# An attention and feed-forward kernel whose order is a table of times: two entries moved by a fifth of a pair

## The chip, the cores and the metric

The kernel runs on one core of one Trainium2 chip. The metric is the device time of one execution in microseconds (us); the runs of the kernel before took 1797.93, 1798.88 and 1799.62, median 1798.88. A further execution of it was profiled; the trace is of that one.

The engines of the core are called PE (TensorE, the matrix unit; PEld is its loading of weights), VectorE or DVE, ScalarE or ACT, GpSimd or POOL, and SyncE or SP, which issues the transfers. Each works through its own instructions in the order in which the program issued them, and waits where an operand or a buffer is not ready.

## What is computed

`x` holds 4 batches of 12480 tokens of 128 features. The first step is attention of 32 learned points over all tokens of a batch, the second is attention of the tokens over the 32 results, and the third is a feed-forward with a squared ReLU of width 2048.

```python
def mab(q, kv):
    s = scale * (q @ kv.transpose(0, 2, 1))
    s = s - s.max(-1, keepdims=True)
    a = np.exp(s)
    a /= a.sum(-1, keepdims=True) + 1e-09
    return a @ kv
h = mab(I, x)
attn = mab(x, h)
...
h = np.maximum(attn @ w_in, 0.0)
return (h * h @ w_out)
```

## The kernel before

The tokens of a batch come in 13 *units* of 960, each in two *blocks* of 480. A block goes through the feed-forward in eight *pairs* of 128-wide slices of the 2048. For each pair of a block (function `ffn_block`, line numbers of the profile):

- `wide` (L508): two matmuls into `h` in PSUM, from `hw`, the product of the attention's result and `w_in`, and `st`, the attention weights.
- `relu` (L515) and `square` (L522) on ScalarE make `r` and then `g`, 128 x 960.
- `high` (L593 on VectorE, L595 on GpSimd) rounds `g` to `hi`, in the PE's reduced float32; the table `HI` says which engine does it for which pair. For one pair in sixteen it says "f": that pair is not split.
- `low` (L530) on VectorE subtracts: `lo` = `g` - `hi`.
- `narrow` (L543): six matmuls add into `op` in PSUM: `hi` by `wo_hi` twice, `hi` by `wo_lo` twice, `lo` by `wo_hi` twice. The pair that is not split has two full float32 products of `g` by `wo_f` in their place.

After a block's last pair, `done` copies `op` to `ot` (VectorE, L593), `turn` transposes it on PE into `otp` (L569), `turned` scales it into `osb` (VectorE, L577), and after the second block `osb` is sent out.

Between these the attention runs ahead. Of the next unit, the second attention: `s` (PE, L420), `ss`, `s2t` (PE, L432), `mx`, `d` (VectorE, L443), the exponential on ScalarE, `sk` (GpSimd and VectorE), and `ap` (PE, L477), which becomes `st`. Of the next batch, the first attention: `xtp` (PE, L263), `sp` (L278), `ep` (L312), `hp` (L324). In a batch's last unit `first_end` joins the first attention's results and makes `hw` of the next batch out of four products `wp` (PE, L393). The last batch has no first attention beside it. All the small PE results share two PSUM banks (`bank`), which go round: the second `wp` takes the bank that `s2t` had, once `d` has read it.

Nothing is scheduled by a tool. Each step is entered in a list with a time on a clock that counts pairs, the list is sorted, and the steps are issued in that order:

```python
t = t0 + p
for i in range(2):
    at(t + AT_G1 + 0.01 * i, lambda i=i: wide(i))
at(t, relu)
...
    at(t + AT_HI[HI[k][p]], high)
    at(t + AT_LO, low)
for j in range(len(steps)):
    at(t + AT_G2 + AT_G2D * j * (6 // len(steps)), lambda j=j: narrow(j))
...
end = t0 + NP - 1 + AT_G2 + 6 * AT_G2D
```

So the table's numbers set no times on the chip; they only set which instruction stands ahead of which on its engine. The buffers go round as well: three of `r` and `lo`, four of `g` and `hi`, two of `h`.

Of the kernel before, what the change touches and what calls it, by code (L numbers as in the profile page):

```python
# [18 lines left out]
PSUM = bass.MemoryType.PSUM  # L19

P = 128
TS = 120          # tokens of a sub-tile
NT = 8            # sub-tiles of a unit
UNIT = TS * NT    # tokens of a unit
BLK = UNIT // 2   # tokens of a block, the width of the feed-forward products


@with_exitstack
def induced_attention_then_squared_relu_ffn(
# [9 lines left out]
    B, N, C = x.shape  # L39
# [3 lines left out]
    NP = NF // 2  # L43
    NU = N // UNIT
    Q = P // M
    scale = 1.0 / math.sqrt(C)
    # engines, by pair of f-tiles in the first and the second block of a unit; "f": not split
    SQ = ('aaaaaaaa', 'aaaaaaaa')   # of the square
    HI = ('vpvpvvpf', 'vvpvvpvv')   # of the rounding
    # engines that empty PSUM  # L50
    XT, XT_EARLY, ET, SS, ST, OT = 'av', 'aa', 'a', 'v', 'av', 'vv'
    RB, GB, HB, LB = 3, 4, 4, 3
    AT_G1, AT_SQA, AT_SQV, AT_HIP, AT_HIA, AT_HIV, AT_LO, AT_G2, AT_G2D = -1.4, 1.05, 0.8, 1.1, 0.7, 1.2, 2.05, 3.3, 0.16
    AT_HI = {"p": AT_HIP, "a": AT_HIA, "v": AT_HIV}
    T_START = (-0.2, 0.3, 0.6, 0.7, 1.5, 1.7, 2.0, 2.4, 3.2, 3.3, 4.1, 4.5)
    T_MAIN = (1.1, 2.2, 2.9, 4.2, 7.2, 7.7, 8.02, 10.3, 10.5, 11.1, 13.4, 13.5)
# [20 lines left out]
    def bank(name):  # L77
        return ps_m.tile([P, 512], F32, tag="m", name=name)

    # token p * (N / TS) + j of a batch lies on partition p of sub-tile j  # L80
    x_v = x.rearrange("b (p j) c -> b p j c", p=TS)
    out_v = out.rearrange("(b p j) c -> b p j c", b=B, p=TS)

    def load_x(b, u, pool):
        xn = pool.tile([TS, NT, C], F32, tag="xn", name=f"xn_{b}_{u}")
        nc.sync.dma_start(xn, x_v[b, :, u * NT:(u + 1) * NT, :])
        return xn
# [4 lines left out]
    make_identity(nc, ident)  # L92
    identr = const.tile([P, P], F32R, name="identr")
    nc.vector.tensor_copy(identr, ident)
    # same_m[(q m), (k m')] = (m == m')
    same_m = const.tile([P, Q, M], F32, name="same_m")
    nc.vector.tensor_reduce(
        same_m[:, 0, :], ident.rearrange("p (q m) -> p m q", q=Q), axis=AX.X, op=ALU.add
# [2 lines left out]
        nc.vector.tensor_copy(same_m[:, k, :], same_m[:, 0, :])  # L101

    same = same_m.rearrange("p k m -> p (k m)")
    # lane_q[(q m), q'] = (q == q')
    lane_q = const.tile([P, Q], F32, name="lane_q")
    nc.vector.tensor_reduce(
        lane_q, ident.rearrange("p (q m) -> p q m", q=Q), axis=AX.X, op=ALU.add
# [6 lines left out]
    indT = const.tile([C, M], F32, name="indT")  # L114
    nc.vector.tensor_copy(indT, it_ps[:C, :M])

# [1 line left out]
    plan = []  # L118

    def at(t, fn):  # L120
# [2 lines left out]
    w_in_sb = const.tile([C, F], F32, name="w_in_sb")  # L123
    wo_hi = const.tile([P, NF, C], F32R, name="wo_hi")
    wo_lo = const.tile([P, NF, C], F32R, name="wo_lo")
    # w_out's tiles for the products that are not split
    FULL = [p for p in range(NP) if "f" in (HI[0][p], HI[1][p])]
    wo_f = const.tile([P, 2 * max(len(FULL), 1), C], F32, name="wo_f")

# [3 lines left out]
    ABOVE = float(np.array(1151 << 20, np.int32).view(np.float32))  # L133

    def weights(name, load, use, t0, step):
        """Steps that turn float64 weights, as words (low, high), into float32 parts (a, b).

        a has the leading 21 bits and b the rest; what float32 has no exponent for becomes 0 or
        infinite, as a cast would have it: a high word's order as a float32 is that of its exponent.
        """  # L140
        v = {}
        shape = [P, WCH]

        def tile_of(tag, dtype):
            return pools["stage"].tile(shape, dtype, tag=tag, name=f"{tag}_{name}")

        def words():
            v["w"] = pools["stage"].tile([P, WCH, 2], I32, tag="words", name=f"words_{name}")
            load(v["w"])

        def clamp():
            v["hc"] = tile_of("hc", F32)
            nc.vector.tensor_scalar(
                v["hc"], v["w"][:, :, 1].bitcast(F32), ABOVE, -ABOVE, ALU.min, ALU.max
            )

        def size():
            v["m"] = tile_of("m", F32)
            nc.scalar.activation(v["m"], v["hc"], AF.Abs)

        def flush():
            nc.vector.scalar_tensor_tensor(v["hc"], v["m"], LEAST, v["hc"], ALU.is_ge, ALU.mult)

        def field():
            v["a"] = tile_of("a", I32)
            nc.vector.tensor_scalar(
                v["a"], v["hc"].bitcast(I32), 3, 0x3FFFFFF8,
                ALU.logical_shift_left, ALU.bitwise_and,
            )

        def sign():
            nc.vector.scalar_tensor_tensor(
                v["a"], v["hc"].bitcast(I32), -0x40000000, v["a"], ALU.bitwise_and, ALU.bitwise_or
            )

        def power():
            v["power"] = tile_of("m", I32)
            nc.vector.tensor_single_scalar(v["power"], v["a"], -0x800000, ALU.bitwise_and)

        def low():  # L180
            v["b"] = tile_of("b", F32)
            nc.vector.scalar_tensor_tensor(
                v["b"], v["w"][:, :, 0].bitcast(U32), 2.0 ** -52, v["power"].bitcast(F32),
                ALU.mult, ALU.mult,
            )
            use(v["a"].bitcast(F32), v["b"])

        at(t0 - 1.5, words)
        for i, fn in enumerate((clamp, size, flush, field, sign, power, low)):
            at(t0 + step * i, fn)  # L190
# [4 lines left out]
        pools["stage"] = pools["scope"].enter_context(tc.tile_pool(name="stage", bufs=2))  # L195

    def open_ffn():
        """The feed-forward takes the place of the weights' staging."""
        pools["scope"].close()
        pools["ffn"] = ctx.enter_context(tc.tile_pool(name="ffn", bufs=3))  # L200

# [38 lines left out]

    state = {}

# [1 line left out]
    # lane (q m): inducing point m over the sub-tiles 2q and 2q + 1 of each unit  # L244
    def first_unit(b, u, t0, ahead, times, early=False):
        v = {}
        n = f"{b}_{u}"
        s = state.setdefault(b, {"xt": []})
# [4 lines left out]
        def turn(k):  # L253
            if k == 0:
                v["xt"] = xt_pool.tile([C, UNIT], F32, tag="xt", name=f"xt_{n}")
                s["xt"].append(v["xt"])
# [5 lines left out]
            for t in range(4):  # L262
                nc.tensor.transpose(  # L263
                    tp[:, t * TS:(t + 1) * TS], v["xn"][:, 4 * k + t, :], ident[:TS, :TS]
                )

        def turned(k):
            part = v["xt"][:, k * BLK:(k + 1) * BLK]
            copy((XT_EARLY if early else XT)[k], part, v["tp"][:, :BLK])

# [14 lines left out]
            nc.vector.tensor_reduce(v["mx"], v["sp"][:, :2 * TS], axis=AX.X, op=ALU.max)  # L285

        def shift():
            # the maximum so far, times -scale
            v["neg"] = tiny.tile([P, 1], F32, tag="neg", name=f"neg_{n}", bufs=4)
            if u:  # L290
                v["before"] = s["neg"]
                nc.vector.scalar_tensor_tensor(
                    v["neg"], v["mx"], -scale, s["neg"], ALU.mult, ALU.min
                )
            else:
                nc.vector.tensor_scalar_mul(v["neg"], v["mx"], -scale)
            s["neg"] = v["neg"]
# [50 lines left out]
            at(t0 + t, fn)  # L348

    def first_end(b, t0, times):  # L350
        """Joins the lanes of each inducing point; h transposed, four times, and h @ w_in split."""
        v = {}
        s = state[b]

# [50 lines left out]
        for t, fn in zip(times, fns):  # L405
            at(t0 + t, fn)

# [1 line left out]
    def second_unit(b, u, t0, times):  # L409
        """The unnormalised weights of a unit's tokens, split in two, as (hi, lo, hi, lo) on partitions."""  # L410
        v = {}
        n = f"{b}_{u}"
        s = state[b]
# [69 lines left out]
        def stacked(k):  # L483
            st = att.tile([P, BLK], F32R, tag="st", name=f"st_{n}_{k}", bufs=4)
            copy(ST[k], st, v["ap"][:, :BLK])
            s["st", u, k] = st
# [5 lines left out]
        for t, fn in zip(times, fns):  # L492
            at(t0 + t, fn)

# [1 line left out]
    def ffn_block(b, u, k, t0):  # L496
        n = f"{b}_{u}_{k}"
        s = state[b]
        w = {}

        def pair(p):
            v = {}

            def wide(i):
                if i == 0:
                    v["hp"] = ps_h.tile([P, 2, 512], F32, tag="h", name=f"h_{n}_{p}")
                f = 2 * p + i
                nc.tensor.matmul(  # L508
                    v["hp"][:, i, :BLK], s["hw"][:, f * P:(f + 1) * P], s["st", u, k],
                    start=True, stop=True,  # L510
                )

            def relu():
                v["r"] = pools["ffn"].tile([P, 2, BLK], F32, tag="r", name=f"r_{n}_{p}", bufs=RB)
                nc.scalar.activation(v["r"], v["hp"][:, :, :BLK], AF.Relu)  # L515
# [57 lines left out]
        def turned():  # L573
            if k == 0:
                s["osb", u] = att.tile([TS, NT, C], F32, tag="osb", name=f"osb_{b}_{u}")
            # block k holds the sub-tiles 2q + k
            nc.vector.tensor_mul(  # L577
                s["osb", u].rearrange("t (q k) c -> t k q c", k=2)[:, k],
                w["tp"][:TS, :].rearrange("t (q c) -> t q c", q=Q),
                s["zz", u][:, k * Q:(k + 1) * Q].broadcast_to([TS, Q, C]),  # L580
            )
            if k == 1:
                nc.sync.dma_start(out_v[b, :, u * NT:(u + 1) * NT, :], s["osb", u])

# [9 lines left out]
        else:  # L594
            nc.gpsimd.tensor_scalar(dst, src, 1.0, 0.0, ALU.mult, ALU.add)  # L595

    # batch 0's first attention, then per batch its blocks and the first attention of the next
    U = 2 * NP
    t_end = START * NU + T_END
    t_main = t_end + T_FFN  # L600
# [52 lines left out]
```

## Time and profile before

| | |
|---|---|
| median of three runs | 1798.88 us |
| span of the profiled execution | 1796.8 us |
| PE busy | 1766.7 us, 98% |
| ScalarE busy | 1628.0 us, 91% |
| VectorE busy | 1620.0 us, 90% |
| GpSimd busy | 442.8 us, 25% |
| mean granted clock of PE | 0.994 |

The span runs from the first to the last instruction; what a run takes beyond it is the start and the end around the program. In a row of the timeline stand the start and the time in us, the engine, the line, the operation, what is written and read (`out<-in`), partitions by elements, and a count; a bracket gives the idle time ahead of it and what ended it. PE's starts are the thing to read: its matmuls overlap, so a matmul's own time is longer than the distance to the next. A row of waits gives the total in us, how often, and the longest.

### The profile page before, as it was taken

The page shows a single profiled execution, that of the slowest core. Times are in us where ns is not written, and L with a number is a line of the kernel's source. Part 1 is how long each engine was busy: PE and PEld are TensorE (multiplying, and loading weights), DVE is VectorE, ACT ScalarE, POOL GpSimd, SP SyncE. Part 2 cuts the span into 40 slices and gives each one's busy share as a digit, 9 for nine tenths or more (in the row PEclk, how much of TensorE's full clock was granted, in tenths as well). Part 3 has the DMA queues.
Part 4 walks back from the last instruction along what each step waited for, and adds up shares of the span by engine and source line. Part 5 has one row for each costly group of instructions (what it writes and reads, how often), then busy time and mean ns, then how long its engine had stood idle before and what let it go on. Part 6 is the DMA issues. An engine that isn't in the chain of part 4 may idle for free.

```text
span 1796.8 us, 27067 instructions
## 1 busy us (share of the span) xinstructions
PE 1766.7 (98%) x9729; PEld 1422.9 (79%) x9729; DVE 1620.0 (90%) x2315; ACT 1628.0 (91%) x2070; POOL 442.8 (25%) x439
## 2 busy tenths in 40 slices
PE   7799999999999999999999999999999999999998
PEld 4478888888778888888878888888887888888887
DVE  6899989999989989989989989989989999999998
ACT  5699999999899999999988999999999999999997
POOL 1312222222222222222221222222222323233231
PEclk9899999999999999999999999999999999999999
DMA  8200100100100110100100110110100000000000
GB/s 214 57 23 23 44 23 23 45 23 23 45 23 23 37 31 23 45 23 23 45 23 23 28 39 23 35 33 23 38 19 12 23 12 23 12 16 19 12 23 23
DMA packets 16912, 57.07 MB, mean 32 GB/s; under 512 B 1704, under 2 KB 3784, under 8 KB 16776
## 3 DMA queue, kind: packets, MB, share of 16 engines
q1 hardware_dynamic: 16776, 55.34, 11.5%
q8 instruction: 76, 1.25, 0.3%
q14 instruction: 60, 0.49, 0.1%
HBM read 29.77 MB, written 25.56 MB: 31 GB/s over the span
## 4 chain that ended last, share of the span: by engine, by line
PE 95%; DVE 2%; DMA 1%; issue 0%; ACT 0%; SPq 0%; POOL 0%; ACTq 0%; DVEq 0%
PE op L543 62%; PE h L508 20%; PE otp L569 3%; PE ap L477 2%; PE xtp L263 2%; PE s L420 2%; PE hp L324 1%; PE sp L278 1%; PE wp L393 1%; DMA words_i<-in_moe_w_in_dram 1%; PE s2t L432 1%; DMA words_o<-in_moe_w_out_dram 1%; PE ep L312 1%; DVE lo L530 0%; DVE mx L285 0%
## 5 line engine op out<-in xcount | busy, mean ns | idle before, releaser
L530 DVE TENSOR_TENSOR lo<-g,hi 128x960 fp32r<-128x960 f32 x780 | 941.9, 1214 | 68.6 <-POOL hi L595 39.1
L515 ACT ACTIVATE r<-h 128x960 f32<-128x960 f32 x832 | 812.0, 976 | 96.8 <-PE h L508 93.7
L522 ACT ACTIVATE g<-r 128x960 f32<-128x960 f32 x832 | 839.6, 1009 | 0.0
L595 POOL TENSOR_SCALAR hi<-g 128x960 fp32r<-128x960 f32 x260 | 282.8, 1088 | 1112.0 <-ACT g L522 1058.1
L543 PE MATMUL op<-hi,wo_hi 128*128 128x480 f32 x1560 | 520.1, 407 | 0.0
L508 PE MATMUL h<-st,hw 128*128 128x480 f32 x1664 | 507.7, 386 | 0.0
L543 PE MATMUL op<-lo,wo_hi 128*128 128x480 f32 x1560 | 479.4, 383 | 0.0
L543 PE MATMUL op<-hi,wo_lo 128*128 128x480 f32 x1560 | 476.2, 381 | 0.0
L593 DVE CAST hi<-g 128x960 fp32r<-128x960 f32 x520 | 374.1, 719 | 3.4 <-ACT g L522 3.4
L543 PEld LDWEIGHTS op<-hi,wo_hi 128*128 128x128 f32 x1560 | 284.4, 189 | 91.7 <-issue 58.7
L508 PEld LDWEIGHTS h<-st,hw 128*128 128x128 f32 x1664 | 306.1, 189 | 47.7 <-issue 3.9
L543 PEld LDWEIGHTS op<-hi,wo_lo 128*128 128x128 f32 x1560 | 293.7, 188 | 43.6
L543 PEld LDWEIGHTS op<-lo,wo_hi 128*128 128x128 f32 x1560 | 293.5, 188 | 41.4 <-DVE lo L530 0.2
L595 POOL TENSOR_SCALAR sk<-d 120x256 fp32r<-120x256 f32 x104 | 102.5, 1001 | 86.3 <-ACT d L446 86.3
L593 DVE COPY ot<-op 128x480 f32<-128x480 f32 x104 | 67.9, 653 | 59.8 <-PE op L543 59.7
L543 PE MATMUL op<-g,wo_f 128*128 128x480 f32 x208 | 100.7, 565 | 0.0
L477 PEld LDWEIGHTS ap<-identr,sk 120*128 120x128 f32 x416 | 62.9, 192 | 26.2 <-issue 20.0
L477 PE MATMUL ap<-identr,sk 120*128 120x120 f32 x416 | 76.3, 306 | 2.0 <-POOL sk L595 2.0
L577 DVE TENSOR_TENSOR osb<-otp,zz 120x512 f32<-120x512 f32 x104 | 70.7, 680 | 2.9 <-PE otp L569 2.2
L263 PE MATMUL xtp<-ident,xn 120*128 120x120 f32 x416 | 63.9, 279 | 8.2 <-DMA xn<-in_x_dram 4.0
L263 PEld LDWEIGHTS xtp<-ident,xn 120*128 120x128 f32 x416 | 51.2, 147 | 22.3 <-ACT xt L591 5.1
L569 PE MATMUL otp<-ident,ot 128*120 128x128 f32 x416 | 63.8, 276 | 0.8 <-DVE ot L593 0.8
(89 smaller groups left out, 867.3 us busy)
## 6 DMA issues: line engine op xcount, KB each, us to landing
xn<-in_x_dram SPq DMA_DIRECT2D x52, 480.0 KB, 5.7
out_dram<-osb SPq DMA_DIRECT2D x52, 480.0 KB, 3.7
words_i<-in_moe_w_in_dram SPq DMA_DIRECT2D x4, 512.0 KB, 6.7
words_o<-in_moe_w_out_dram SPq DMA_DIRECT2D x4, 512.0 KB, 5.0
ind_sb<-in_inducing_dram SPq DMA_DIRECT2D x1, 16.0 KB, 1.7
```

Source lines behind the costliest of these rows:

```text
L263: nc.tensor.transpose(tp[:, t * TS:(t + 1) * TS], v["xn"][:, 4 * k + t, :], ident[:TS, :TS])
L420: nc.tensor.matmul(sp[q * M:(q + 1) * M, :2 * TS], s["hT"][:, :M], xt[:, q * 2 * TS:(q + 1) * 2 * TS], start=True, stop=True,)
L477: nc.tensor.matmul(ap[:, q * TS:(q + 1) * TS], v["sk"][:, k * Q + q].rearrange("t a k m -> t (a k m)"), identr[:TS, :TS], start=(q == 0), ...
L508: nc.tensor.matmul(v["hp"][:, i, :BLK], s["hw"][:, f * P:(f + 1) * P], s["st", u, k], start=True, stop=True,)
L515: nc.scalar.activation(v["r"], v["hp"][:, :, :BLK], AF.Relu)
L522: nc.scalar.activation(v["g"], v["r"], AF.Square)
L530: nc.vector.tensor_sub(v["lo"], v["g"], v["hi"])
L543: nc.tensor.matmul(w["op"][:, :BLK], wo[:, f, :], v[part][:, i, :], start=(p == 0 and j == 0), stop=(p == NP - 1 and j == len(steps) - 1),)
L569: nc.tensor.transpose(tp[:TS, q * P:(q + 1) * P], w["ot"][:, q * TS:(q + 1) * TS], ident)
L577: nc.vector.tensor_mul(s["osb", u].rearrange("t (q k) c -> t k q c", k=2)[:, k], w["tp"][:TS, :].rearrange("t (q c) -> t q c", q=Q), s["zz ...
L593: nc.vector.tensor_copy(dst, src)
L595: nc.gpsimd.tensor_scalar(dst, src, 1.0, 0.0, ALU.mult, ALU.add)
```

## The change

Two numbers of the table move by 0.2, a fifth of a pair: `AT_LO`, the place of `low`, and `AT_G2`, the place of the first of the `narrow` products, with which the other five and the end of a block (`done`, `turn`, `turned`) move too. The comments that the diff also takes out have no effect.

```diff
-    AT_G1, AT_SQA, AT_SQV, AT_HIP, AT_HIA, AT_HIV, AT_LO, AT_G2, AT_G2D = -1.4, 1.05, 0.8, 1.1, 0.7, 1.2, 2.05, 3.3, 0.16
+    AT_G1, AT_SQA, AT_SQV, AT_HIP, AT_HIA, AT_HIV, AT_LO, AT_G2, AT_G2D = -1.4, 1.05, 0.8, 1.1, 0.7, 1.2, 2.25, 3.5, 0.16
```

The rounding of the next pair stands at 1 + 1.1 = 2.1 (GpSimd) or 1 + 1.2 = 2.2 (VectorE) of a pair's clock, so `low` goes from just ahead of it to just behind it. The `h` products of the third pair after it stand at 3.6, so they go from behind the second `narrow` product (3.46) to ahead of it (3.66). On ScalarE, GpSimd and SyncE the order is the same in both kernels.

VectorE, in an ordinary unit of the last batch, pairs 3 to 6 of a first block; names end in unit, block, pair and a running number. Before:

```order
L530 TENSOR_TENSOR lo_5_0_3_17196<-g_5_0_3_17181,hi_5_0_3_17184 128x960
L593 CAST hi_5_0_4_17201<-g_5_0_4_17198 128x960
L577 TENSOR_TENSOR osb_4_17054<-otp_4_1_17209,zz_4_16638 120x4x128
L530 TENSOR_TENSOR lo_5_0_4_17224<-g_5_0_4_17198,hi_5_0_4_17201 128x960
L450 TENSOR_REDUCE z_3_6_17228<-d_6_17175 120x8
L593 CAST hi_5_0_5_17231<-g_5_0_5_17226 128x960
L530 TENSOR_TENSOR lo_5_0_5_17243<-g_5_0_5_17226,hi_5_0_5_17231 128x960
L469 TENSOR_TENSOR sk_6_17205<-d_6_17175,sk_6_17205 120x8x32
```

The same stretch in the changed kernel:

```order
L530 TENSOR_TENSOR lo_5_0_3_17200<-g_5_0_3_17178,hi_5_0_3_17180 128x960
L577 TENSOR_TENSOR osb_4_17054<-otp_4_1_17212,zz_4_16637 120x4x128
L450 TENSOR_REDUCE z_3_6_17225<-d_6_17173 120x8
L593 CAST hi_5_0_5_17228<-g_5_0_5_17223 128x960
L530 TENSOR_TENSOR lo_5_0_4_17230<-g_5_0_4_17195,hi_5_0_4_17198 128x960
L469 TENSOR_TENSOR sk_6_17204<-d_6_17173,sk_6_17204 120x8x32
L530 TENSOR_TENSOR lo_5_0_5_17248<-g_5_0_5_17223,hi_5_0_5_17228 128x960
```

`lo` of pair 4 stands behind `z` and the rounding of pair 5 now, `lo` of pair 5 behind `sk`; the rounding of pair 4 has gone ahead of `lo` of pair 3.

PE, in an ordinary unit of the second batch, second block, where `hp` and `otp` stand. Before:

```order
L543 MATMUL op_5_1_7932<-hi_5_1_1_7900,wo_hi 128x480 x2
L508 MATMUL h_5_1_6_7954<-st_5_1_7570,hw_5477 128x480 x2
L543 MATMUL op_5_1_7932<-hi_5_1_1_7900,wo_lo 128x480 x2
L543 MATMUL op_5_1_7932<-lo_5_1_1_7922,wo_hi 128x480 x2
L543 MATMUL op_5_1_7932<-hi_5_1_2_7926,wo_hi 128x480
L324 MATMUL hp_6_7970<-xn_6_7438,et_6_7928 32x128 x8
L569 MATMUL otp_5_0_7979<-ident,ot_5_0_7930 120x128 x4
L543 MATMUL op_5_1_7932<-hi_5_1_2_7926,wo_hi 128x480
L508 MATMUL h_5_1_7_7989<-st_5_1_7570,hw_5477 128x480 x2
```

And in the changed kernel:

```order
L543 MATMUL op_5_1_7932<-hi_5_1_1_7897,wo_hi 128x480
L508 MATMUL h_5_1_6_7953<-st_5_1_7568,hw_5475 128x480 x2
L543 MATMUL op_5_1_7932<-hi_5_1_1_7897,wo_hi 128x480
L543 MATMUL op_5_1_7932<-hi_5_1_1_7897,wo_lo 128x480 x2
L543 MATMUL op_5_1_7932<-lo_5_1_1_7928,wo_hi 128x480 x2
L324 MATMUL hp_6_7969<-xn_6_7435,et_6_7926 32x128 x8
L543 MATMUL op_5_1_7932<-hi_5_1_2_7924,wo_hi 128x480
L508 MATMUL h_5_1_7_7983<-st_5_1_7568,hw_5475 128x480 x2
L569 MATMUL otp_5_0_7986<-ident,ot_5_0_7930 120x128 x4
L543 MATMUL op_5_1_7932<-hi_5_1_2_7924,wo_hi 128x480
```

The two `h` products stand between the two products of `hi` by `wo_hi`; `hp` and `otp` are parted by three matmuls, and `otp` stands behind the `h` products.

PE, where the first batch ends and the second begins, from `wp_0` to the transposes behind it. Before:

```order
L543 MATMUL op_12_0_5496<-lo_12_0_1_5487,wo_hi 128x480 x2
L393 MATMUL wp_0_5539<-w_in_sb,hT_5475 128x512
L543 MATMUL op_12_0_5496<-hi_12_0_2_5492,wo_hi 128x480
L569 MATMUL otp_11_1_5542<-ident,ot_11_1_5494 120x128 x4
L543 MATMUL op_12_0_5496<-hi_12_0_2_5492,wo_hi 128x480
L508 MATMUL h_12_0_7_5548<-st_12_0_5268,hw_865 128x480 x2
```

And in the changed kernel:

```order
L543 MATMUL op_12_0_5496<-lo_12_0_1_5491,wo_hi 128x480
L393 MATMUL wp_0_5538<-w_in_sb,hT_5473 128x512
L543 MATMUL op_12_0_5496<-lo_12_0_1_5491,wo_hi 128x480
L543 MATMUL op_12_0_5496<-hi_12_0_2_5489,wo_hi 128x480
L508 MATMUL h_12_0_7_5542<-st_12_0_5265,hw_865 128x480 x2
L569 MATMUL otp_11_1_5545<-ident,ot_11_1_5494 120x128 x4
L543 MATMUL op_12_0_5496<-hi_12_0_2_5489,wo_hi 128x480
```

`otp` has the two `h` products ahead of it. The second product `wp_1`, further down, has only one of the two products of `hi` of pair 5 ahead of it, where it had both.

## The prediction

> **What bounds the kernel now.** I read the page first: its table of busy shares, its chain and its costliest groups.
>
> ```profile
> PE 1766.7 (98%) x9729; PEld 1422.9 (79%) x9729; DVE 1620.0 (90%) x2315; ACT 1628.0 (91%) x2070; POOL 442.8 (25%) x439
> PE 95%; DVE 2%; DMA 1%; issue 0%; ACT 0%; SPq 0%; POOL 0%; ACTq 0%; DVEq 0%
> L530 DVE TENSOR_TENSOR lo<-g,hi 128x960 fp32r<-128x960 f32 x780 | 941.9, 1214 | 68.6 <-POOL hi L595 39.1
> L593 DVE CAST hi<-g 128x960 fp32r<-128x960 f32 x520 | 374.1, 719 | 3.4 <-ACT g L522 3.4
> ```
>
> TensorE (PE) is the chain: 95% of the span. A busy 98% alone would prove little, since ends of matmuls are modelled, so I asked next for PE's waits on other engines, from 100 us on:
>
> ```profile
> PE wp L393 <- DVE d L443: 1.3, 2, 0.6
> PE otp L569 <- DVE ot L593: 0.8, 1, 0.8
> ```
>
> These are all: 2.1 us in three places. Two lie where one batch ends and the next begins (at `wp`), one is the last transpose of the program. So the time moves only if PE's own row of matmuls gets longer or shorter, if one of the three waits grows, or if a wait appears where there is none today.
>
> **The change part by part.** On ScalarE, GpSimd and SyncE the order of instructions stays as it was. VectorE and PE change. Their work is the same; nothing is added or taken away.
>
> *VectorE.* The subtraction `lo` of pair p now stands behind the rounding `hi` of pair p+1: it ends about one CAST later (719 ns). PE asks for `lo` at the same place in its row as before. So what counts is how long `lo` lies ready today. The tightest units are those of the last batch. The timeline there, VectorE, then GpSimd, then PE:
>
> ```profile
> 1584.01 0.67 DVE L577 TENSOR_TENSOR osb<-otp,zz 120x512 f32<-120x512 f32 x1
> 1584.60 1.14 DVE L530 TENSOR_TENSOR lo<-g,hi 128x960 fp32r<-128x960 f32 x1
> 1585.66 0.41 DVE L450 TENSOR_REDUCE z<-d 120x8 f32<-120x256 f32 x1
> 1585.99 0.65 DVE L593 CAST hi<-g 128x960 fp32r<-128x960 f32 x1
> 1586.75 1.75 DVE L530 TENSOR_TENSOR lo<-g,hi 128x960 fp32r<-128x960 f32 x1
> ...
> 1586.02 1.47 POOL L595 TENSOR_SCALAR hi<-g 128x960 fp32r<-128x960 f32 x1 [1.68 <-ACT g L522]
> ...
> 1582.94 0.60 PE L569 MATMUL otp<-ident,ot 128*120 128x128 f32 x4
> 1587.74 0.59 PE L543 MATMUL op<-lo,wo_hi 128*128 128x480 f32 x2
> 1589.48 0.60 PE L543 MATMUL op<-lo,wo_hi 128*128 128x480 f32 x2
> ```
>
> `lo` of pair 4 is ready at 1584.60 + 1.14 = 1585.74 and used at 1587.74: 2.00 us to spare. Now `z` and `hi` of pair 5 stand ahead of it. By the starts of these rows `osb` takes 0.59, `z` 0.33 and `hi` 0.76, so it starts at 1584.01 + 1.68 = 1585.69. It then meets GpSimd's rounding at 1586.02, as `lo` of pair 5 does today, whose 1.75 stands for 1.14; with 1.75 it ends at 1587.44, and 0.30 is left. `lo` of pair 5 comes behind it and `sk` (about 0.35), at 1587.8, ends at 1588.95 and is used at 1589.48. So nothing is late in an ordinary unit, by this sum, but one `lo` has only 0.30 us of cover left, and without it PE pays the lateness once in every unit.
>
> `hi` itself comes earlier. What could stop it is its ring of four buffers, which PE must have read; the whole trace has one such wait, of GpSimd:
>
> ```profile
> POOL hi L595 <- PE op L543: 5.7, 1, 5.7
> ```
>
> I cost that at nothing: the products that free a buffer keep their place in PE's row.
>
> *PE, in its row of matmuls.* The two `h` products now stand between the two products of `hi` with `wo_hi` and not behind them. Three kinds of neighbours change beside that. First, `hp` and `otp` stood side by side in 28 units and already stood apart in the later units of the third batch. The trace prices that: the same piece of five products recurs once per unit in the chain.
>
> ```profile
> 699.30 1.51 PE op L543 x5
> 832.90 1.51 PE op L543 x5
> 1138.77 1.51 PE op L543 x5
> 1305.98 1.51 PE op L543 x5
> ```
>
> Side by side, four units took 133.60, or 33.40 each; apart, five took 167.21, or 33.44. So it is 0.042 us a unit. After the change all stand apart: 28 x 0.042 = 1.2 us. The rows of one such unit show where it lies: `otp` follows `hp` without a product of the feed-forward between.
>
> ```profile
> 806.51 0.64 PE L324 MATMUL hp<-xn,et 120*32 120x128 f32 x16
> 807.09 0.65 PE L569 MATMUL otp<-ident,ot 128*120 128x128 f32 x4
> ```
>
> The Trainium skill (TensorE: Matmul & The Clock Gate, Part 2: What happens when you issue a matmul) has PE pull a weight load ahead of matmuls in flight when it goes to the background buffer or other row groups; read broadly, a change of neighbours would then cost nothing, and the sum would be 1.6 us lower with it and the next item. The trace's 33.40 against 33.44 speaks against the broad reading here.
>
> Second, `xtp` and `s2t` are parted in 35 units. No row prices it. It lies between 0 and the same 0.042 (0 to 1.5 us); I take 0.4, nearer nothing, since neither has the 32-column weights of `hp`. Third, the second `ap` of a unit moves from behind the first unsplit product to ahead of it, 48 times. It may cost or gain; I bound it by 0.04 either way (2.0 us) and take 0.
>
> *PE, the rhythm of a pair.* The eight matmuls of an undisturbed pair do not always take the same time. Starts of `h` from the timeline:
>
> ```profile
> 807.80 0.60 PE L508 MATMUL h<-st,hw 128*128 128x480 f32 x2
> 809.55 0.59 PE L508 MATMUL h<-st,hw 128*128 128x480 f32 x2
> 811.30 0.59 PE L508 MATMUL h<-st,hw 128*128 128x480 f32 x2
> 815.95 0.60 PE L508 MATMUL h<-st,hw 128*128 128x480 f32 x2
> 817.68 0.60 PE L508 MATMUL h<-st,hw 128*128 128x480 f32 x2
> ```
>
> 1.75 in one stretch, 1.73 in the other, and nothing in the trace says why. I take the mix to stay, 0, and keep half of 0.02 either way for all 780 pairs (the count of `lo`): 7.8 us up or down.
>
> *The batch boundaries.* Here the existing wait grows. The chain of the first one, and the transpose ahead of it:
>
> ```profile
> 485.44 0.60 PE L569 MATMUL otp<-ident,ot 128*120 128x128 f32 x4
> ...
> 486.08 0.69 DVE osb L577
> 491.51 1.06 DVE lo L530
> 492.63 0.34 DVE d L443
> 493.11 1.10 PE wp L393 x2
> ```
>
> From `osb` to `d` the chain runs on VectorE: osb waits for `otp`, `wp` waits for `d`. Now two products `h` stand ahead of `otp`, about 0.22 each (1.75 / 8), so `osb` and `d` come 0.43 later. VectorE has the same instructions in between, in another order. And one product that stood ahead of `wp` stands behind it: 0.22 more. 0.65 at each of two boundaries, 1.3 us; the third has no wait here and I leave it at 0. If VectorE caught up, it would be as little as 0.
>
> *The end.* VectorE again goes without a gap from `osb`, which waits for a transpose, to the last `lo`:
>
> ```profile
> 1782.58 0.69 DVE L577 TENSOR_TENSOR osb<-otp,zz 120x512 f32<-120x512 f32 x1 [0.23 <-PE otp L569]
> 1786.67 1.16 DVE L530 TENSOR_TENSOR lo<-g,hi 128x960 fp32r<-128x960 f32 x1
> 1787.74 0.65 DVE L593 CAST hi<-g 128x960 fp32r<-128x960 f32 x1
> 1788.50 1.16 DVE L530 TENSOR_TENSOR lo<-g,hi 128x960 fp32r<-128x960 f32 x1
> 1788.45 0.59 PE L543 MATMUL op<-lo,wo_hi 128*128 128x480 f32 x2
> 1789.75 0.67 PE L543 MATMUL op<-lo,wo_hi 128*128 128x480 f32 x2
> ```
>
> That transpose stands two products later, 0.43. `lo` of pair 6 was ready at 1787.83; now it is 0.43 later and has the last `hi` ahead of it (0.76 by the starts): 1789.02, and PE wants it at 1788.45. PE waits 0.6 us. The last `lo` ends at 1790.09, and PE, itself 0.57 later, asks at 1790.32. Without the wait ahead of osb it would be 0.2; I take 0.6.
>
> *Sum.* 1.2 + 0.4 + 0 + 0 + 1.3 + 0.6 = 3.5 us. The profiled span is 1796.8 and the median of the runs 1798.88, so 2.1 lie around the span: 1796.8 + 3.5 + 2.1 = **1802.4 us**, slower by 0.2%. About 0.2% (3.6 us) is what a measurement of this kernel can tell from no change, so this forecast stands on that line.
>
> **The rivals.** (A) PE waits for `lo` in ordinary units. For it: 0.30 us is left, and that after a contention that today makes 1.75 of 1.14. Against: PE has no such wait today, and 0.91 is left where GpSimd keeps away. It decides when `lo` of pair 4 ends later than 1587.74. At 0.3 late in the 12 units of the last batch: 3.6 us, 1806.0. The Trainium skill (SBUF — State Buffer, SBUF: two separate sides) calls the port pair that VectorE and GpSimd share an exclusive lock: a VectorE instruction with two SBUF inputs, which `lo` is, or GpSimd's blocks the other for its whole length. By that rule `lo` behind GpSimd's 1.47 would start at 1587.49 and be 0.89 late, 10.7 us in the 12 units, 1813.1; the rows above agree only in that `lo` grows, by 0.6. Chance of all of (A): 0.18.
>
> (B) The pairs fall into the quick rhythm, all 780: 1802.4 - 7.8 = 1794.6, faster by 0.24%. For it: 1.73 stands in the trace, and the new order is another row of weights. Against: both rhythms stand in one unit with one order. It decides from half of the pairs on that change. Chance 0.10; the same into the slow rhythm gives 1810.2, chance 0.05.
>
> (C) The waits are covered: VectorE makes up its 0.43 at the boundaries, and the parted neighbours cost what they cost together. Then it is 1798.9, or up to 1800. For it: VectorE is idle for a tenth of the span. Against: the two boundary chains have no gap. Chance 0.17.
>
> **How the numbers follow.** My forecast has 0.50, half of it on either side of the line. Slower by over 0.2%: 0.25 + 0.18 + 0.05 = 0.48. Within 0.2%: 0.25 + 0.17 = 0.42. Faster: 0.10. The range reaches from C, with the gain of 2.0 at `ap` half taken, 1797.5, to A with the slow rhythm's first quarter on top, 1808.0; B's end and the far slow end stay out.
>
> **What would show it.** Units of the first two batches at 33.44 to 33.48 and not 33.40; the wait of `wp` for `d` 0.4 to 0.65 longer at two boundaries; a wait of PE for the second last `lo`; no wait of PE for `lo` in ordinary units. It is wrong if such waits appear there (A), if units come out shorter than 33.40 (B), or if the boundary waits stay at 1.3 us (C).

## The result and the profile after

The changed kernel took 1808.37 us (median of four runs, 1806.95 to 1810.63), the kernel before 1799.16 beside it. The ratio is 1.0054, with an interval of 1.004 to 1.0069: slower by 0.5%, or 9.2 us. The prediction's 1802.4 is 6 us short, and its range ended at 1808.0.

The page of the changed kernel, in its table of busy shares, its chain and its groups:

```profile
PE 1775.6 (98%) x9729; PEld 1421.7 (79%) x9729; DVE 1624.2 (90%) x2315; ACT 1633.0 (90%) x2070; POOL 466.8 (26%) x439
PE 94%; DVE 3%; DMA 1%; ACT 1%; issue 1%; SPq 0%; POOL 0%; ACTq 0%; DVEq 0%
L530 DVE TENSOR_TENSOR lo<-g,hi 128x960 fp32r<-128x960 f32 x780 | 929.2, 1197 | 0.5
```

TensorE is still the chain, and it is busy 9 us longer with the same 9729 matmuls. Its granted clock is 1.00 in every stage from 100 to 1790 us in both kernels, so the clock has no part in this. VectorE gained: one `lo` costs 1197 ns, 1214 before. The waits of PE from 100 us on:

```profile
PE wp L393 <- DVE d L443: 1.3, 2, 0.7
PE ap L477 <- DVE hacc L339: 0.9, 2, 0.4
PE otp L569 <- DVE ot L593: 0.8, 1, 0.8
PE sp L278 <- DVE hw L400: 0.5, 2, 0.3
```

There is no wait for `lo`. Two waits are new, for `hacc` and `hw`, each twice: 1.4 us in all. The other 8 us of 9.2 are not waits; they are in the row of matmuls. The timeline shows where: starts of `h`, four units apart, in the second batch and in the last.

```profile
548.36 0.60 PE L508 MATMUL h<-st,hw 128*128 128x480 f32 x2
...
682.71 0.60 PE L508 MATMUL h<-st,hw 128*128 128x480 f32 x2
...
1426.37 0.60 PE L508 MATMUL h<-st,hw 128*128 128x480 f32 x2
...
1550.21 0.60 PE L508 MATMUL h<-st,hw 128*128 128x480 f32 x2
```

Four units take 134.35 in the second batch (133.60 before) and 123.84 in the last (123.52 before, by the same starts of `h`). I added up all units from one start of `h` to the next, from the second unit of the program to the end:

| part | before | after | difference, all of them |
|---|---|---|---|
| ordinary units, batches 1 and 2 (22) | 33.402 mean | 33.586 mean | +4.04 us |
| ordinary units, batch 3 (11) | 33.40 to 33.45 | 33.54 to 33.59 | +1.45 |
| ordinary units, batch 4 (11) | 30.880 | 30.960 | +0.88 |
| first unit behind a boundary (3) | 33.85, 33.85, 31.36 | 34.03, 34.05, 31.45 | +0.46 |
| boundary units (3) | 38.14, 38.17, 34.55 | 39.28, 39.28, 34.58 | +2.28 |
| last unit and end | | | +0.19 |

That is 9.3 us, what the medians say. The profiled execution (1810.63) has some 2.7 us more ahead of this: its first `h` starts at 73.42, before at 70.03, and its first unit is 0.7 shorter. The later start is not the change's: up to there both kernels run the same instructions in the same order on every engine, and over the profiles of all fourteen kernels here the first `h` started anywhere from 69.5 to 73.4.

### The profile page after: what moved, and what is told of

The parts are those of the page before. It is cut to its first block, busy times and chain, and to the rows that moved or that the text cites. A ratio compares the mean times of both kernels' runs of the same rounds, so it can differ in the third digit from the quotient of the medians.

```text
span 1808.9 us, 27421 instructions
## 1 busy us (share of the span) xinstructions
PE 1775.6 (98%) x9729; PEld 1421.7 (79%) x9729; DVE 1624.2 (90%) x2315; ACT 1633.0 (90%) x2070; POOL 466.8 (26%) x439
## 4 chain that ended last, share of the span: by engine, by line
PE 94%; DVE 3%; DMA 1%; ACT 1%; issue 1%; SPq 0%; POOL 0%; ACTq 0%; DVEq 0%
PE op L543 61%; PE h L508 20%; PE otp L569 2%; PE ap L477 2%; PE xtp L263 2%; PE s L420 2%; PE hp L324 1%; PE sp L278 1%; DVE lo L530 1%; DMA words_i<-in_moe_w_in_dram 1%; PE wp L393 1%; PE s2t L432 1%; DMA words_o<-in_moe_w_out_dram 1%; PE ep L312 0%; ACT r L515 0%
## 5 line engine op out<-in xcount | busy, mean ns | idle before, releaser
L530 DVE TENSOR_TENSOR lo<-g,hi 128x960 fp32r<-128x960 f32 x780 | 929.2, 1197 | 0.5
L543 PE MATMUL op<-hi,wo_hi 128*128 128x480 f32 x1560 | 628.6, 403 | 0.0
L595 POOL TENSOR_SCALAR hi<-g 128x960 fp32r<-128x960 f32 x260 | 309.9, 1192 | 1135.7 <-ACT g L522 839.8
L543 PE MATMUL op<-lo,wo_hi 128*128 128x480 f32 x1560 | 506.3, 392 | 0.0
L593 DVE CAST hi<-g 128x960 fp32r<-128x960 f32 x520 | 348.1, 669 | 81.8 <-ACT g L522 75.5
L508 PEld LDWEIGHTS h<-st,hw 128*128 128x128 f32 x1664 | 310.3, 189 | 65.2 <-issue 19.4
L543 PEld LDWEIGHTS op<-lo,wo_hi 128*128 128x128 f32 x1560 | 289.5, 188 | 71.2 <-issue 33.4
L543 PEld LDWEIGHTS op<-hi,wo_hi 128*128 128x128 f32 x1560 | 294.0, 188 | 58.8 <-issue 20.0
L595 POOL TENSOR_SCALAR sk<-d 120x256 fp32r<-120x256 f32 x104 | 71.9, 709 | 89.6 <-ACT d L446 89.6
L595 POOL TENSOR_SCALAR sk<-sk 120x256 fp32r<-120x256 f32 x52 | 64.2, 1235 | 52.7 <-DVE sk L469 52.3
```

Source lines behind the costliest of these rows:

```text
L508: nc.tensor.matmul(v["hp"][:, i, :BLK], s["hw"][:, f * P:(f + 1) * P], s["st", u, k], start=True, stop=True,)
L530: nc.vector.tensor_sub(v["lo"], v["g"], v["hi"])
L543: nc.tensor.matmul(w["op"][:, :BLK], wo[:, f, :], v[part][:, i, :], start=(p == 0 and j == 0), stop=(p == NP - 1 and j == len(steps) - 1),)
L593: nc.vector.tensor_copy(dst, src)
```

## The experiments

I had the theory, called N, that the loss is made in PE's row: a block of the attention (`xtp`, `sp`, `hp`, `ap`, `otp`) costs more between some products than between others. The rival, D, was that the later `lo` costs it, by waits or by VectorE's accesses. R says that the inner order of a pair costs by itself. Two more came later: I, that moving a block is dear only with the new inner order, and S, that a block also sets how long the pairs behind it take. Four units are always counted from the same starts of `h` as above.

**1. AT_LO alone.**

```diff
-    ... AT_LO, AT_G2, AT_G2D = ... 2.05, 3.3, 0.16
+    ... AT_LO, AT_G2, AT_G2D = ... 2.25, 3.3, 0.16
```

> AT_LO 2.25 alone; AT_G2 stays 3.3. TensorE's row is that of the kernel before, VectorE has each subtraction behind the next rounding. Theory N (the loss is made in TensorE's own row, where blocks of attention now stand between other products): units of the first two batches stay at 33.400 us, the total within 1 us of before, and only the boundary units (38.14) may grow, by at most 1.1 each. Theory D (the loss comes from the later subtraction: waits, or VectorE's accesses slowing TensorE's): units near 33.587, total about 1805 to 1808.

Ratio 1.0005 (0.9995 to 1.0014). The starts of `h`, and the waits:

```profile
541.85 0.59 PE L508 MATMUL h<-st,hw 128*128 128x480 f32 x2
...
675.45 0.59 PE L508 MATMUL h<-st,hw 128*128 128x480 f32 x2
```

```profile
PE ap L477 <- DVE hacc L339: 0.9, 2, 0.5
PE wp L393 <- DVE d L443: 0.7, 2, 0.4
```

133.60, as before, and each pair takes what it took before within 2 ns, but for the boundary units and the units behind them. So D falls for the ordinary units, where 6.8 of the 9.2 us lie. The wait for `hacc` is here without the change on PE; it belongs to the later `lo`. The boundary units are 38.61, up by 0.45.

At the end of the program `lo` does come too late here, which PE's waits do not list because the waiting stands at the weight load ahead of the product:

```profile
1788.60 0.30 PEld L543 LDWEIGHTS op<-lo,wo_hi 128*128 128x128 f32 x2 [0.46 <-DVE lo L530]
```

The products with this `lo`, the second last, start 0.2 us late. That is most of the 0.26 that the end costs here.

**2. AT_G2 alone.**

```diff
-    ... AT_LO, AT_G2, AT_G2D = ... 2.05, 3.3, 0.16
+    ... AT_LO, AT_G2, AT_G2D = ... 2.05, 3.5, 0.16
```

> AT_G2 3.5 alone; AT_LO stays 2.05. TensorE's row is that of the changed kernel, VectorE subtracts as early as before. Theory N: units of 33.587 in the first two batches and 30.960 in the last, total 1806 to 1808. Theory D: units of 33.40, total 1799 to 1800. The two new boundary waits (ap for hacc, 0.4 each; sp for hw, 0.3) stay under the theory that they come from TensorE's row and go if the subtractions ahead of hacc and hw on VectorE make them.

Ratio 1.0053 (1.0036 to 1.007).

```profile
547.33 0.60 PE L508 MATMUL h<-st,hw 128*128 128x480 f32 x2
...
681.68 0.60 PE L508 MATMUL h<-st,hw 128*128 128x480 f32 x2
```

```profile
PE sp L278 <- DVE hw L400: 2.1, 2, 1.1
```

```profile
492.13 1.45 DVE L593 CAST hi<-g 128x960 fp32r<-128x960 f32 x1
```

134.35, the whole loss of an ordinary unit, with VectorE's order as before. The wait for `hw` belongs to this half, up to 1.1 at a boundary; the full change has 0.3. The last row, of VectorE ahead of `hw`, says why: this rounding takes 1.45 here, and in the full change, where it stands ahead of the `lo`, 0.65 (shown below). The boundary units are 39.41 and 39.43, and the third, where the full change has 34.58, is 35.29. Together they cost 3.26 us here, more than the 2.28 of the full change: at the boundaries the later `lo` gives back part of what the later products cost.

**3. The attention a fifth of a pair later as well**, which puts the blocks back between nearly the same products.

```diff
-    AT_S2, AT_S1 = 0.05, 0.05
+    AT_S2, AT_S1 = 0.25, 0.25
```

> The changed kernel with all steps of the attention a fifth of a pair later as well (AT_S2, AT_S1 0.25). Then the blocks of the attention stand between the same products as before (xtp and sp behind the second lo, xtp and s2t together, the second ap behind g1, hp and otp together); only h stands between the two products of hi. Theory N: most of the 0.187 us a unit goes, units of 33.40 to 33.46, total 1799 to 1802. Theory R (the rhythm of the pairs with h inside the two hi is what costs): units stay near 33.55 and more, total about 1806 to 1808.

Ratio 1.0042 (1.0027 to 1.0057).

```profile
546.50 0.61 PE L508 MATMUL h<-st,hw 128*128 128x480 f32 x2
...
680.59 0.61 PE L508 MATMUL h<-st,hw 128*128 128x480 f32 x2
```

134.09, or 33.52 a unit, so 0.26 of 0.75 goes. This is neither N nor R: the pairs with `xtp` are cheap again (2.165, before 2.156, changed kernel 2.200), but undisturbed pairs that took 1.740 take 1.760.

**4. The transposes of the output back at their old time.**

```diff
-    O_MAIN = (0.0, 2.2, 2.5)
+    O_MAIN = (0.0, 2.0, 2.3)
```

> The changed kernel with the transposes of the output put back to their old time (O_MAIN 0.0, 2.0, 2.3): otp stands right behind hp again, both between the second lo and the first hi, and the other otp of the unit between the same two. Theory N: 0.059 us a unit less where hp and otp were together before (28 units, 1.7 us), units near 33.53, total about 1806.5. If the parting of hp and otp is not what costs, units stay within 0.01 of 33.587. At the boundaries osb comes earlier by about 0.43, and the waits for hacc and hw shrink if they follow from otp, by up to 0.8 in all.

Ratio 1.0051 (1.0036 to 1.0066).

```profile
546.36 0.61 PE L508 MATMUL h<-st,hw 128*128 128x480 f32 x2
...
680.56 0.61 PE L508 MATMUL h<-st,hw 128*128 128x480 f32 x2
```

134.20, 0.037 a unit less, not 0.059. The two pairs with `hp` and `otp` gave their 0.064 (4.663 for 4.727), but other pairs moved as well, some up by 0.02 (1.760 for 1.740). In the last batch the same edit made a unit longer, 31.02 for 30.96. The boundary units went to 38.68 and 38.70 and the wait for `hw` vanished: it hangs on `otp`.

**5 and 6. One product of each pair moved**, to part the inner order from the places of the blocks. In the fifth the kernel before gets the second product of `hi` behind `h`; in the sixth the changed kernel gets it back ahead of `h`. One place does not part cleanly: `otp` stood next to the product that moves, so in the fifth it has `h` behind it, and in the sixth the first product by `wo_lo`.

```diff
-                at(t + AT_G2 + AT_G2D * j * (6 // len(steps)), lambda j=j: narrow(j))
+                late = 0.155 if j == 1 and not full else 0.0
+                at(t + AT_G2 + AT_G2D * j * (6 // len(steps)) + late, lambda j=j: narrow(j))
```

> The kernel before with one product of each pair moved: the second product of hi with wo_hi stands behind the two h, as in the changed kernel, while every block of the attention stays between the same other products and VectorE keeps its order. Theory N (each block pays for its place, and the places add): units of the first two batches at 33.40, at most 0.02 more, total 1799 to 1800. Theory R (the inner order of the pair costs by itself, as the units of 33.52 with the attention shifted too suggest): 33.50 to 33.53, total 1803 to 1805.

```diff
-                at(t + AT_G2 + AT_G2D * j * (6 // len(steps)), lambda j=j: narrow(j))
+                early = 0.07 if j == 1 and not full else 0.0
+                at(t + AT_G2 + AT_G2D * j * (6 // len(steps)) - early, lambda j=j: narrow(j))
```

> The changed kernel with that one product put back ahead of the two h: the inner order of the pair is that of the kernel before, the blocks of the attention stand at their new places, VectorE is as in the changed kernel. Theory N: units stay at 33.57 to 33.60, total 1807 to 1808. Theory R: most of the loss in ordinary units goes, units at 33.40 to 33.47, total 1801 to 1803, with the boundary units still near 39.28.

Ratios 1.0008 (0.9998 to 1.0017) and 1.0028 (1.0017 to 1.0039). The starts of `h` in the fifth, then in the sixth:

```profile
542.56 0.60 PE L508 MATMUL h<-st,hw 128*128 128x480 f32 x2
...
676.17 0.60 PE L508 MATMUL h<-st,hw 128*128 128x480 f32 x2
```

```profile
543.69 0.60 PE L508 MATMUL h<-st,hw 128*128 128x480 f32 x2
...
677.53 0.60 PE L508 MATMUL h<-st,hw 128*128 128x480 f32 x2
```

133.61 and 133.84, beside 133.60 with neither and 134.35 with both. Per unit the new inner order costs 0.003, the new places cost 0.06, and both together 0.187. The fifth came out as N had it and the sixth as R had it, so neither theory stands: the costs do not add. The last batch, which has no first attention beside it, is another case. There four units take 123.52 before, 123.89 with the new inner order alone, 123.48 with the new places alone and 123.84 with both: its whole loss comes with the inner order. The sixth's boundary units, at 39.47, keep their loss.

**7 and 8. One block moved by one product in the kernel before:** `xtp` in the seventh, `hp` in the eighth.

```diff
-    T_MAIN = (1.1, 2.2, ...
+    T_MAIN = (0.95, 2.2, ...
```

> The kernel before with one block of each unit moved by one product: the first xtp stands between the two products of lo and not behind them. In the changed kernel the pair with this block takes 2.200 us instead of 2.156. Theory N: that pair takes 2.200 and the others what they took, units 33.444, total up by 1.7 us (39 units). Theory S (a block sets the rhythm of the pairs behind it, until the next block): pairs behind it change as well, between 1.731 and 1.760 each, and the unit's sum is not 33.444 but anywhere from 33.38 to 33.50.

```diff
-    T_MAIN = (... 13.4, 13.5)
+    T_MAIN = (... 13.2, 13.5)
```

> The kernel before with the other block moved by one product: hp stands ahead of the first product of hi and not behind it, so hp and otp are parted by that product. In the changed kernel the two pairs with hp and otp take 4.727 us instead of 4.668 or 4.655. Theory N: units 33.46, total up by 1.7 us (28 units). Theory S: the two pairs change by another amount and the undisturbed pairs behind them change too; the unit's sum is anywhere from 33.38 to 33.50. My prediction's own price for the parting, 0.042, would give 33.44.

Ratios 1.0003 (0.9993 to 1.0013) and 1.001 (1.0001 to 1.0019). Seventh, then eighth:

```profile
544.28 0.59 PE L508 MATMUL h<-st,hw 128*128 128x480 f32 x2
...
677.88 0.59 PE L508 MATMUL h<-st,hw 128*128 128x480 f32 x2
```

```profile
542.60 0.59 PE L508 MATMUL h<-st,hw 128*128 128x480 f32 x2
...
676.36 0.59 PE L508 MATMUL h<-st,hw 128*128 128x480 f32 x2
```

`xtp` between the two `lo` products costs nothing here (133.60; its pair 2.160, not 2.200), while other pairs of the unit moved, one down by 0.02 to 0.03 and the next one up by 0.019. `hp` parted from `otp` costs 0.16 in four units, 0.040 each: the prediction's 0.042.

**9 to 12. The same with the new inner order.** The base is the fifth kernel (133.61); each moves one kind of block to where the changed kernel has it.

```diff
-    T_MAIN = (1.1, 2.2, ...
+    T_MAIN = (0.95, 2.2, ...
```

> The kernel of the fifth experiment (the second hi product behind the two h; units 33.403) with the first xtp of each unit one product earlier, between the two products of lo, as in the changed kernel. The order of the old kernel took this move for nothing (units 33.400). Theory I (the move is dear only with h inside the two hi products): the pair with xtp goes from 2.163 to 2.200, units 33.44, total up by 1.5 us on that kernel. Theory S (what a pair takes hangs on the state in which the row of matmuls comes to it, set by all blocks of the unit together): the pair takes 2.16 to 2.175 here, and units stay within 0.02 of 33.403.

```diff
-    T_MAIN = (... 13.4, 13.5)
+    T_MAIN = (... 13.2, 13.5)
```

> The kernel of the fifth experiment with hp one product earlier, ahead of the first hi product, so that hp and otp are parted by it. In the old order this move cost 0.040 a unit. Theory I: 0.06 or more here (changed kernel: 4.727 for the two pairs, 4.641 to 4.658 in the fifth), units 33.46 and up. Theory S: the place alone gives about the 0.040 of the old order, units near 33.44, and the rest of the 0.187 needs the other blocks.

```diff
-    S_MAIN = (... 9.52, 9.6, 10.1, 10.3, 11.9)
+    S_MAIN = (... 9.52, 9.562, 10.1, 10.2, 11.9)
```

> The kernel of the fifth experiment with both ap of each unit where the changed kernel has them (the first between h and the second hi, the second ahead of the first unsplit product). Theory I: the two pairs go from 4.881 to 4.911, units 33.43. Theory S: anything from 33.38 to 33.46, with undisturbed pairs behind them changed too. My prediction had this place at nothing, within 0.04.

```diff
-    O_MAIN = (0.0, 2.2, 2.5)
+    O_MAIN = (0.0, 2.353, 2.653)
```

> The kernel of the fifth experiment with both otp of each unit two products later, between the two h and the second hi product, as in the changed kernel; hp stays behind the first hi product. Theory I: hp and otp parted cost 0.04 to 0.06 a unit, units 33.44 to 33.46. Theory S: the pairs behind otp change between 1.740 and 1.760 too, units anywhere from 33.40 to 33.55. At the boundaries osb is 0.43 later: if that alone makes wp wait for d, as my prediction had it, the boundary units grow by 0.6 each; if they stay within 0.1 of 38.06, the step from otp to that wait is wrong.

Ratios 1.0015 (1.0006 to 1.0024), 1.0036 (1.0023 to 1.005), 1.0012 (1.0002 to 1.0021) and 1.0049 (1.0034 to 1.0064), all against the kernel before. Starts of `h` with `xtp` moved, then `hp` (its third row is the next pair), then `ap`, then `otp`:

```profile
541.41 0.60 PE L508 MATMUL h<-st,hw 128*128 128x480 f32 x2
...
675.17 0.60 PE L508 MATMUL h<-st,hw 128*128 128x480 f32 x2
```

```profile
541.92 0.60 PE L508 MATMUL h<-st,hw 128*128 128x480 f32 x2
...
675.94 0.61 PE L508 MATMUL h<-st,hw 128*128 128x480 f32 x2
677.70 0.61 PE L508 MATMUL h<-st,hw 128*128 128x480 f32 x2
```

```profile
542.37 0.60 PE L508 MATMUL h<-st,hw 128*128 128x480 f32 x2
...
676.09 0.60 PE L508 MATMUL h<-st,hw 128*128 128x480 f32 x2
```

```profile
545.21 0.61 PE L508 MATMUL h<-st,hw 128*128 128x480 f32 x2
...
679.39 0.61 PE L508 MATMUL h<-st,hw 128*128 128x480 f32 x2
```

133.76, 134.02, 133.72 and 134.18: a unit costs 0.037, 0.10, 0.027 and 0.14 more. (The units of the second kernel are not all alike; over all 22 of them `hp` costs 0.114.) `xtp` goes from 0 to 0.037 and `hp` from 0.040 to 0.10 by nothing but the inner order of the pairs. Theory I has the direction, but its sizes for `xtp` come out at the wrong place: the pair with `xtp` takes 2.161, as little as in the fifth kernel, and pairs behind it pay, the next two among them (1.748 and 2.384 for 1.738 and 2.372). That is what S says; S's own numbers, 33.42 and 33.44 at most for the first two, were too low. Over all 22 units the four steps add up to 0.32, while the changed kernel, with all four and more, stands only 0.18 above the fifth. No version here beats the kernel before, and none of the runs points to one by more than can be measured.

The last kernel also answers for the boundaries: with `otp` later and nothing else, the boundary units are 39.18 (fifth kernel 38.06). Its waits:

```profile
PE sp L278 <- DVE hw L400: 1.8, 2, 0.9
PE wp L393 <- DVE d L443: 1.5, 2, 0.7
```

The wait for `d` hardly moves (1.3 in the fifth kernel); the new one is for `hw`.

## Why the prediction was wrong

**What bounds the kernel** held: PE's row and PE's waits on VectorE account for all of it.

**VectorE** held, and with more to spare than the 0.30 us. Pairs 4 and 5 of a unit in the changed kernel's last batch, VectorE, GpSimd, then PE:

```profile
1596.58 0.65 DVE L593 CAST hi<-g 128x960 fp32r<-128x960 f32 x1
1597.14 1.15 DVE L530 TENSOR_TENSOR lo<-g,hi 128x960 fp32r<-128x960 f32 x1
1599.34 1.15 DVE L530 TENSOR_TENSOR lo<-g,hi 128x960 fp32r<-128x960 f32 x1
...
1597.33 1.82 POOL L595 TENSOR_SCALAR hi<-g 128x960 fp32r<-128x960 f32 x1 [1.45 <-ACT g L522]
...
1599.35 0.59 PE L543 MATMUL op<-lo,wo_hi 128*128 128x480 f32 x2
1601.09 0.60 PE L543 MATMUL op<-lo,wo_hi 128*128 128x480 f32 x2
```

`lo` of pair 4 ends at 1598.29 and is used at 1599.35: 1.06 us to spare. The tightest of an ordinary unit is now pair 5, with 0.60; the prediction's sum gave it 0.53. The prediction let `lo` of pair 4 meet GpSimd's rounding and take 1.75. They do meet, but now `lo` starts first, takes its 1.15, and GpSimd's rounding is the one that grows, to 1.82. By the prediction's own starts (1585.69 against 1586.02) `lo` came first as well, so the 1.75 was carried over from a meeting of the other kind. In that one, in the prediction's rows, `lo` starts second and ends 1.01 behind the rounding (1588.50 and 1587.49).

Rival (A) falls with that. Its 1813.1, by the exclusive lock of the Trainium skill (SBUF — State Buffer, SBUF: two separate sides), had `lo` waiting behind GpSimd, and the trace has it the other way round. The prediction found its rows to agree with that lock only in that `lo` grows. Both its rows and the ones above agree further: the one that starts later ends a fixed time behind the other, with the numbers in the last section.

**PE's row** is the step that failed: "Three kinds of neighbours change beside that", with a price of 0.042, 0.4 in all, and 0. It came to 1.6 us; the ordinary units and those behind a boundary cost 4.04 + 1.45 + 0.88 + 0.46 = 6.8. The changed kernel, pair by pair, in a unit of the second batch:

| pairs of a unit | before | after |
|---|---|---|
| with the first `xtp` | 2.156 | 2.200 |
| with `xtp` and `s2t` | 2.373 | 2.387 |
| with both `ap` (two pairs) | 4.853 or 4.867 | 4.911 |
| with `hp` and `otp` (two pairs) | 4.655 or 4.668 | 4.727 |
| the other ten together, with `s`, `sp` and the other `otp` | 19.335 or 19.363 | 19.361 |

So 0.17 of 0.187 shows in the pairs with blocks, and my bound for one block, 0.042, was passed by the pairs with `ap` and by those with `hp` and `otp`. I also overlooked that the first `xtp`, `s` and `sp`, which had stood behind both `lo` products, now part them; `xtp` alone shows 0.044 there. But a longer list with local prices would have failed too. The price of 0.042 was right for the row that it came from: the eighth experiment measures 0.040 in the old order. In the new order the same move costs 0.10 to 0.11 (tenth). A price read off one order does not hold in another. And the new place of the two `h` products, between the two of `hi` with `wo_hi`, had no price but the 0 of the rhythm below. In the last batch just this costs 0.08 to 0.09 a unit (fifth experiment, 123.89 for 123.52 in four units).

The Trainium skill (TensorE: Matmul & The Clock Gate, Part 2: What happens when you issue a matmul) lets PE load weights ahead of matmuls in flight, which read broadly makes neighbours free. The seventh experiment agrees, with 0 for a moved `xtp`; the eighth (0.040), the tenth (0.10) and the twelfth (0.14) do not.

**The rhythm of a pair** I left at 0, "I take the mix to stay", with 7.8 us either way. The pairs without those blocks did stay by themselves, the ten others above by 0.012 on average. Yet the rhythm and the blocks hang together: what a block costs shows in part in the pairs behind it (fourth, ninth and tenth experiment). Two separate terms, one priced and one left at 0, could not give the sum.

**The boundaries** were mis-sized, 1.3 for 2.28, and their place was wrong. VectorE and PE at the first one, in the changed kernel:

```profile
490.80 0.60 PE L569 MATMUL otp<-ident,ot 128*120 128x128 f32 x4
...
491.43 0.69 DVE L577 TENSOR_TENSOR osb<-otp,zz 120x512 f32<-120x512 f32 x1 [0.96 <-PE otp L569]
492.04 0.65 DVE L593 CAST hi<-g 128x960 fp32r<-128x960 f32 x1
492.61 1.15 DVE L530 TENSOR_TENSOR lo<-g,hi 128x960 fp32r<-128x960 f32 x1
493.79 0.69 DVE L400 TENSOR_TENSOR hw<-wp,hw 64x512 fp32r<-64x512 f32 x1
...
494.54 0.61 PE L278 MATMUL sp<-xt,indT 128*32 128x240 f32 x8 [0.27 <-DVE hw L400]
...
511.09 1.15 DVE L530 TENSOR_TENSOR lo<-g,hi 128x960 fp32r<-128x960 f32 x1
512.27 0.29 DVE L339 COPY hacc<-hp 128x128 f32<-128x128 f32 x1
...
512.71 0.63 PE L477 MATMUL ap<-identr,sk 120*128 120x120 f32 x4 [0.44 <-DVE hacc L339]
```

The chain from `otp` through `osb` is the one that the prediction followed to `d` and `wp`. On its way lies `hw`, which reads the first `wp`; `sp`, which takes one of the two banks, waits until that is done: 0.27. PE itself is then late, so `wp` waits no longer than before (1.3 in all). The other new wait comes from the later `lo`: one stands ahead of `hacc` now, which reads `hp`, and `ap`, for its bank, waits 0.44. The first experiment shows the one, the second and the twelfth the other. Of the 1.12 a boundary, 0.71 is idle time in these two rows; the rest was not taken apart.

**The end** was wrong in kind: no wait for the second last `lo`. It cost 0.2, not 0.6, and that was not taken apart. The wait came only in the first experiment, where `lo` alone is later.

Of the signs that I named, one came (no wait for `lo` in ordinary units); units of 33.44 to 33.48, the longer wait of `wp` and a wait at the end did not. One sum of the prediction is off by itself: the low end of its range, C with half of the 2.0 at `ap` gained, is 1797.9 and not 1797.5, which decides nothing.

## What to carry to other kernels

Where matmuls follow each other without a gap, a change of their order alone can cost time, here 6.8 of 9.2 us, with every wait covered. A price for one neighbour, read from the trace of one order, does not bound it in another, so give the whole row one wide term and measure. Where a result on another engine comes later, follow every reader along the chain, not only the one that waits today: the first on the way can take the wait.

## What the runs showed of the hardware

Eight matmuls in the same order take from 1.737 to 1.760 us, most often 1.740, depending on what stood ahead of them. In the rows of the tenth experiment the pair from 675.94 to 677.70 takes 1.76. In the fifth the same eight products in the same order go from 676.17, shown above, to the next row:

```profile
677.91 0.60 PE L508 MATMUL h<-st,hw 128*128 128x480 f32 x2
```

1.74. Only the place of `hp`, two pairs ahead, differs between these two kernels. The lengths recur to 1 to 2 ns in every unit of an order, and often alternate between two values from unit to unit (33.394 and 33.413 in the fifth kernel), though the order is the same. When VectorE's times alone changed (first and second experiment against the kernels with the same row of matmuls), they did not move in the ordinary units. So the row on PE carries a state from one block to the next that its order sets. What that state is, none of the runs shows: a weight load lasts 188 ns in each, as in this group of the changed kernel's page (busy time, then the mean of one in ns),

```profile
L543 PEld LDWEIGHTS op<-lo,wo_hi 128*128 128x128 f32 x1560 | 289.5, 188 | 71.2 <-issue 33.4
```

and the starts of these matmuls lie 0.21 to 0.225 apart in all the rhythms.

The state also shows right behind a block: between the start of the first product behind `otp` and that of the next one lie 0.306 us or 0.324, with the same instructions around them, in two pairs of one unit of the changed kernel.

VectorE's `lo` and GpSimd's rounding do not share their time: where they meet, the first to start keeps its own time and the other ends a fixed time later. In the changed kernel `lo` starts first 83 times, takes 1.14 to 1.16 us, and the rounding ends 0.85 to 0.87 behind it, whatever the distance of the starts; alone it takes 0.99. Where the rounding starts 0.08 us or more ahead of one `lo`, in 50 places, `lo` ends 1.00 to 1.01 behind it; alone it takes 1.15. In two places the rounding started by only 0.02 earlier, and `lo` kept its time all the same.
